# Another order of the first group's front in an attention and max-out kernel

## The chip, the cores and the metric

The kernel runs on one core of one Trainium2 chip. The metric is the device time of one execution in microseconds, from runs of the same compiled program; the median of the runs shown is compared. A profile of one execution lists each engine's instructions: TensorE (PE, with its weight loads as PEld), VectorE (DVE), ScalarE (ACT), GpSimd (POOL) and SyncE (SP), whose queue issues the transfers.

## The reference

q, k and v have the shape 8 x 8 x 576 x 64 (batch, heads, sequence, head size) in 32-bit floats. Attention is taken within chunks of 64 positions, and its output feeds a layer that takes the larger of three products:

```python
scores = scale * np.matmul(q_c, k_c.transpose(0, 1, 2, 4, 3))   # per chunk of 64
scores = scores - np.max(scores, axis=-1, keepdims=True)
attn = np.exp(scores)
attn = attn / (np.sum(attn, axis=-1, keepdims=True) + 1e-09)
out = np.matmul(attn, v_c)
x = out.transpose(0, 2, 1, 3).reshape(4608, 512)
h = np.maximum(np.maximum(x @ w1, x @ w2), x @ w3)              # w1..w3: 512 x 768
y = h @ w_out                                                   # w_out: 768 x 512
```

## The kernel before

The 4608 rows of x are cut into 36 tiles of 128 rows. Tiles 0 to 3 are the first group, 4 to 7 the second, and four units of 6, 8, 8 and 6 tiles follow. Matrix products are made from a high and a low part of each operand: three products (low x high, high x low, high x high, lines 187 to 189) add up in a bank of PSUM. The weights come in as 64-bit words and are converted on the chip into such a high and a low part.

The order of the first group's work, and of the second group's beginning, is written out by hand in the string `FIRST` (line 45). `first_group` walks through it and calls, for each name, the function that issues those instructions. An engine runs its own instructions in the order of the string; between engines the program puts waits where one reads or overwrites what another has written. What comes after the string is placed by a planner with due times, and by loops over the units.

The names, with t for a tile and jw for a piece of the weights (j is a block of 128 columns of the hidden layer, w one of the three matrices):

- `Wjw`, `qt`, `vt`: transfers on SP's queue. `Wjw` loads a piece of weights (512 KB), `qt` loads q and k of tile t (512 KB), `vt` its v (256 KB). A load waits until its buffer is free: q0, q3 and others share three buffers, `v0` and `v2` share one, as do `v1` and `v3`.
- `Ajw`, `Bjw`, `Cjw`, `Xjw`, `Hjw`, `Yjw`: the conversion of a piece. A (line 163) and B (line 168) run on ScalarE, C (line 172, a shift) on VectorE, X (line 176, an integer addition of what B and C left) on VectorE or, with a `p` behind the name, on GpSimd, H (line 179, the high part) on ScalarE, Y (line 182, the low part) on VectorE or, with `p`, on GpSimd.
- `St`: 32 products of 64 x 64 on TensorE, the scores of tile t (line 237). `mxt` (line 242) and `subt` (line 247) on VectorE take the maximum out of PSUM and subtract it; `expt` (line 251) runs on ScalarE; `sumt` (line 195), `epst` (line 198, adds 1e-9) and `rect` (line 201, the reciprocal) run on VectorE; `nrmt` (line 204) multiplies on VectorE or, with `p`, on GpSimd.
- `Tt`: four transposes on TensorE (line 260); `att` copies them on ScalarE (line 265); `Vt` multiplies with v on TensorE (line 296); `xht` (ScalarE, line 303) and `xlt` (VectorE, line 307) write the tile's high and low part of x.
- `hjwa`, `hjwb`, `hjwf`: twelve products of x with the converted piece, for the columns of tiles 0 and 1 (a), 2 and 3 (b) or all four (f). They need H and Y of the piece, and xh and xl of the tiles. `Fjwa` and so on (lines 349 and 351) take the larger of the results.
- `in`: n idle products on zeroed operands (line 795). They compute nothing that is used.

The scores of two tiles lie in one tile of PSUM, the outputs of V in another, with the tile's number inside and the half of the chunk outside:

```python
banks_of[name] = ps[name].tile([P, 2, 2, 4, 64], F32, name=name[-1])
st["s"] = s = bank_of("ps_s")[:, :, t % 2 if t < 4 or "pair" in st else 0]
```

so a tile's scores lie in both of its banks, in each beside those of the other tile. The pieces' words are placed by the order of the names in `FIRST`: `words_in` and `values_in` (lines 125 to 138) hand out rooms as W and A come, and take them back as X and Y come.

Of the kernel before, what the change touches and what calls it, by code (L numbers as in the profile page):

```python
# [42 lines left out]


FIRST = """
q0 i13 W01 A01 S0 i5 mx0 q1 sub0 W00 C01 exp0 sum0 S1 mx1 sub1 B01 q2 A00 exp1 W12 eps0 v0 q3 i8 rec0 B00 X01p S2 sum1
H01 mx2 eps1 nrm0p T0 at0 rec1 v1 sub2 nrm1p V0 T1 exp2 C00 S3 X00p xh0 q4 W02 at1 B12 sum2 H00 eps2 V1 rec2 mx3 xh1
nrm2p sub3 T2 S4 xl0 exp3 xl1 sum3 at2 Y00p v2 B02 W10 eps3 rec3 v3 nrm3 A02 W20 h00a V2 A12 C02 W31 T3 Y01p A10 xh2
X02 H02 at3 C10 W11 C12 X12p F00a h01a Y02 V3 xl2 B10 xh3 B31 q5 X10p xl3 A20 W21 A11 h02a F01a H12 F02a B11 C11 W61
W52 Z B20 B21 W40 H10 mx4 sub4 hh0a exp4 W22 C20 X20 W32 Y12 X11 Y10 A31 H11 W30 h01b hl0a h00b C31 h02b A21 H20 X31  # L50
S5 F00b C21 Y11 h12f F01b A40 q6 v4 H31 sum4 W41 B40 X21p h10f F02b H21 Y31 Y20 B30 hh0b eps4 hl0b Y21 C40 mx5 B61
X40p h11f h20f B32 F10f rec4 A22 sub5 W42 A32 C32 S6 A30 X32p h21f B22 W64 F11f F12f W51 C22 B52 H40 hh1f nrm4 hl1f
# [969 lines left out]
```

## Time and profile before

| | |
|---|---|
| median of 3 runs | 612.15 us (610.98 to 612.55) |
| profiled execution | 613.47 us |
| its span, first to last instruction | 611.7 us |
| TensorE busy | 600.5 us, 98% of the span |
| VectorE busy | 421.6 us, 69% |
| ScalarE busy | 290.4 us, 47% |
| GpSimd busy | 187.5 us, 31% |
| mean granted TensorE clock | 0.999 |
| transferred | 148.95 MB, mean 243 GB/s |

A row of a timeline gives the start in us from the span's start, the duration in us, the engine, the line of the kernel, the operation, what it writes and reads with the shapes, and how many instructions the row merges; in brackets stands the idle time of the engine ahead of it and what ended that. A row of the busy times by stretches gives the stretch, its length, then the busy time and the number of instructions of PE, PEld, DVE, ACT and POOL, the granted TensorE clock, the share of time in which the DMA engines were busy, and GB/s. A row of the transfers gives what is loaded, the queue, the count, the size, and the time from issue to landing in us.

### The profile page before, as it was taken

The numbers are of one execution on the slowest core, as the hardware profiler recorded it, in microseconds if no ns is written. First come the engines' busy times: TensorE is split into PE (matmuls) and PEld (weight loads), VectorE is DVE, ScalarE is ACT, GpSimd is POOL, SyncE is SP. The second block draws the span as 40 slices with busy tenths as digits, with TensorE's granted clock in tenths as the row PEclk, the third lists the DMA queues.
The fourth block names the chain that finished last, engine by engine and source line by source line (L and its number), as shares of the span: only waits on it lengthen the run. The fifth ranks groups of instructions, "written<-read, shape, count | busy, mean of one in ns | idle before, by whom it ended". The sixth has DMA issues, their size and how long they took to land.

```text
span 611.7 us, 12712 instructions
## 1 busy us (share of the span) xinstructions
PE 600.5 (98%) x5046; PEld 521.1 (85%) x5046; DVE 421.6 (69%) x700; ACT 290.4 (47%) x522; POOL 187.5 (31%) x168
## 2 busy tenths in 40 slices
PE   7899999999999999999999999999999999999997
PEld 3788878888799999997888878888888888999997
DVE  4898965768977986894674759936465598244373
ACT  4897734443454554555243344643333355333353
POOL 2522477777232424100250512002424000031300
PEclk9999999999999999999999999999999999999999
DMA  8987657755868998747796994468757543677532
GB/s 336 362 310 273 253 190 274 271 204 234 313 227 287 348 333 312 275 134 266 248 313 239 328 289 163 148 235 280 253 193 259 179 155 114 225 253 261 197 129 79
DMA packets 59483, 148.95 MB, mean 243 GB/s; under 512 B 5664, under 2 KB 24608, under 8 KB 59424
## 3 DMA queue, kind: packets, MB, share of 16 engines
q1 hardware_dynamic: 59424, 148.13, 69.0%
q8 instruction: 40, 0.66, 0.4%
q14 instruction: 19, 0.16, 0.1%
HBM read 116.92 MB, written 31.20 MB: 242 GB/s over the span
## 4 chain that ended last, share of the span: by engine, by line
PE 84%; DVE 7%; DMA 3%; ACT 2%; POOL 2%; issue 1%; SPq 0%; DVEq 0%; ACTq 0%; POOLq 0%
PE pm L187 26%; PE pm L189 26%; PE pm L188 26%; PE s L237 2%; PE pm L296 2%; POOL c L420 2%; DMA buf<-in_vb 2%; DMA e<-b 1%; PE tp L260 1%; PE pm L795 1%; DVE e L247 1%; DVE sm L195 1%; DVE s L428 1%; DVE h L361 1%; DVE mx L242 1%
## 5 line engine op out<-in xcount | busy, mean ns | idle before, releaser
L187 PE MATMUL pm<-X,ring 128*128 128x512 f32 (+1 forms) x504 | 184.3, 366 | 0.3 <-ACT kept L626 0.3
L189 PE MATMUL pm<-X,ring 128*128 128x512 f32 (+1 forms) x504 | 182.5, 362 | 0.5 <-issue 0.5
L188 PE MATMUL pm<-X,ring 128*128 128x512 f32 (+1 forms) x504 | 182.4, 362 | 0.0
L626 ACT COPY kept<-pm 128x384 f32<-128x384 f32 (+1 forms) x144 | 76.9, 534 | 156.6 <-PE pm L189 154.9
L187 PEld LDWEIGHTS pm<-X,ring 128*128 128x128 f32 x504 | 94.6, 188 | 11.2 <-ACT kept L626 0.7
L189 PEld LDWEIGHTS pm<-X,ring 128*128 128x128 f32 x504 | 94.6, 188 | 10.7 <-issue 0.8
L188 PEld LDWEIGHTS pm<-X,ring 128*128 128x128 f32 x504 | 94.7, 188 | 9.7
L632 POOL TENSOR_TENSOR kept<-kept 128x384 f32<-128x384 f32 (+1 forms) x24 | 29.0, 1208 | 129.2 <-ACT kept L626 129.2
L629 DVE TENSOR_TENSOR pm<-pm,kept 128x384 f32<-128x384 f32 (+1 forms) x48 | 30.0, 626 | 51.4 <-PE pm L189 51.4
L187 PE MATMUL pm<-xh,wl 128*128 128x512 f32 (+1 forms) x156 | 60.0, 385 | 0.0
L188 PE MATMUL pm<-xl,wh 128*128 128x512 f32 (+1 forms) x156 | 58.4, 374 | 0.3 <-DVE xl L307 0.3
L189 PE MATMUL pm<-xh,wh 128*128 128x512 f32 (+1 forms) x156 | 58.3, 374 | 0.0
L594 DVE TENSOR_TENSOR H<-most,H 128x384 fp32r<-128x384 f32 (+1 forms) x72 | 48.5, 687 | 11.1 <-ACT H L591 11.0
L635 DVE TENSOR_TENSOR most<-pm,most 128x384 f32<-128x384 f32 (+1 forms) x72 | 44.6, 619 | 10.8 <-PE pm L189 9.4
L204 POOL TENSOR_TENSOR e<-e,sm 128x512 f32<-128x512 f32 x27 | 31.3, 1161 | 63.6 <-ACT kept L626 18.9
L242 DVE TENSOR_REDUCE mx<-s 128x8 f32<-128x512 f32 x36 | 24.6, 683 | 36.9 <-PE s L237 36.9
L632 POOL TENSOR_TENSOR most<-kept 128x384 f32<-128x384 f32 (+1 forms) x12 | 13.8, 1150 | 115.8 <-ACT kept L626 115.8
L591 ACT CAST H<-most 128x384 fp32r<-128x384 f32 (+1 forms) x72 | 40.6, 569 | 10.5 <-PE pm L189 9.0
L528 DVE TENSOR_TENSOR X<-stage,X 128x768 fp32r<-128x768 f32 (+1 forms) x28 | 34.0, 1222 | 13.1 <-ACT X L524 13.0
L524 ACT CAST X<-stage 128x768 fp32r<-128x768 f32 (+1 forms) x28 | 26.3, 945 | 28.1 <-DVE stage L519 22.0
L251 ACT ACTIVATE e<-e 128x512 f32<-128x512 f32 x36 | 22.8, 633 | 27.9 <-DVE e L247 27.9
L189 PE MATMUL pm<-H,woh 128*128 128x384 f32 (+1 forms) x96 | 34.7, 362 | 0.0
(119 smaller groups left out, 1062.8 us busy)
## 6 DMA issues: line engine op xcount, KB each, us to landing
ring<-w SPq DMA_DIRECT2D x72, 768.0 KB, 6.0
buf<-in_qk SPq DMA_DIRECT2D x36, 512.0 KB, 6.2
buf<-in_vb SPq DMA_DIRECT2D x36, 256.0 KB, 6.8
ring<-w SPq DMA_DIRECT2D x36, 256.0 KB, 4.1
w<-s SPq DMA_DIRECT2D x9, 768.0 KB, 3.8
out_x<-ao SPq DMA_DIRECT2D x24, 256.0 KB, 3.0
ring<-wo SPq DMA_DIRECT2D x8, 768.0 KB, 5.0
stage<-in_w SPq DMA_DIRECT2D x7, 512.0 KB, 6.4
```

The lines of the kernel that those rows point to most:

```text
L187: nc.tensor.matmul(out=o, lhsT=al, rhs=bh, start=first, stop=False, skip_group_check=shared)
L188: nc.tensor.matmul(out=o, lhsT=ah, rhs=bl, start=False, stop=False, skip_group_check=shared)
L189: nc.tensor.matmul(out=o, lhsT=ah, rhs=bh, start=False, stop=last, skip_group_check=shared)
L204: eng.tensor_tensor(out=e, in0=e, in1=sm.unsqueeze(2).broadcast_to([P, 8, 64]), op=ALU.mult)
L242: nc.vector.tensor_reduce(out=st["mx"].rearrange("p (g c) -> p c g", c=2), in_=st["s"], axis=AX.X, op=ALU.max)
L528: return lambda: eng.tensor_tensor(out=X[i][:, 1], in0=source[i](), in1=X[i][:, 0].bitcast(F32), op=minus)
L591: nc.scalar.copy(out=H[i, jp][:, 0, :half], in_=hidden_block(i, jp))
L594: nc.vector.tensor_tensor(out=H[i, jp][:, 1, :half], in0=hidden_block(i, jp), in1=H[i, jp][:, 0, :half].bitcast(F32), op=minus)
L626: return lambda: nc.scalar.copy(out=to, in_=o)
L629: return lambda: nc.vector.tensor_tensor(out=o if w else M(jp, q), in0=o, in1=kept(k), op=plus)
L632: nc.gpsimd.tensor_tensor(out=kept(3) if w else M(jp, A22), in0=kept(3), in1=kept(p7), op=plus)
L635: return lambda: nc.vector.tensor_tensor(out=M(jp, q), in0=of, in1=M(jp, q), op=most)
```

## The change

The four lines at the head of `FIRST` are written anew; the rest of the string and all functions stay as they are.

```diff
 FIRST = """
-q0 i13 W01 A01 S0 i5 mx0 q1 sub0 W00 C01 exp0 sum0 S1 mx1 sub1 B01 q2 A00 exp1 W12 eps0 v0 q3 i8 rec0 B00 X01p S2 sum1
-H01 mx2 eps1 nrm0p T0 at0 rec1 v1 sub2 nrm1p V0 T1 exp2 C00 S3 X00p xh0 q4 W02 at1 B12 sum2 H00 eps2 V1 rec2 mx3 xh1
-nrm2p sub3 T2 S4 xl0 exp3 xl1 sum3 at2 Y00p v2 B02 W10 eps3 rec3 v3 nrm3 A02 W20 h00a V2 A12 C02 W31 T3 Y01p A10 xh2
-X02 H02 at3 C10 W11 C12 X12p F00a h01a Y02 V3 xl2 B10 xh3 B31 q5 X10p xl3 A20 W21 A11 h02a F01a H12 F02a B11 C11 W61
+W01 q0 i13 A01 B01 q1 C01 X01 W00 H01 Y01 S0 i2 S1 i3 mx0 sub0 q2 A00 exp0 mx1 v0 sum0 eps0 rec0 S2 nrm0p sub1 q3 B00
+exp1 i4 C00 X00p W12 T0 sum1 at0 eps1 rec1 v1 nrm1p S3 H00 mx2 V0 W02 xh0 sub2 T1 exp2 Y00p q4 at1 xl0 mx3 V1 B12 sum2
+xh1 eps2 rec2 nrm2p sub3 xl1 T2 A02 S4 exp3 at2 h00a B02 sum3 v2 C02 W10 eps3 rec3 v3 nrm3 V2 X02 W20 F00a h01a xh2 H02
+T3 A12 W31 xl2 Y02 at3 A10 C10 W11 C12 X12p V3 xh3 B10 B31 q5 X10p xl3 A20 W21 A11 h02a F01a H12 F02a B11 C11 W61
 W52 Z B20 B21 W40 H10 mx4 sub4 hh0a exp4 W22 C20 X20 W32 Y12 X11 Y10 A31 H11 W30 h01b hl0a h00b C31 h02b A21 H20 X31
 S5 F00b C21 Y11 h12f F01b A40 q6 v4 H31 sum4 W41 B40 X21p h10f F02b H21 Y31 Y20 B30 hh0b eps4 hl0b Y21 C40 mx5 B61
 X40p h11f h20f B32 F10f rec4 A22 sub5 W42 A32 C32 S6 A30 X32p h21f B22 W64 F11f F12f W51 C22 B52 H40 hh1f nrm4 hl1f
```

From `B31` on both orders agree. By engine, the orders up to there are these (before, then after):

```
SP    q0 W01 q1 W00 q2 W12 v0 q3 v1 q4 W02 v2 W10 v3 W20 W31 W11
      W01 q0 q1 W00 q2 v0 q3 W12 v1 W02 q4 v2 W10 v3 W20 W31 W11
ACT   A01 exp0 B01 A00 exp1 B00 H01 at0 exp2 xh0 at1 B12 H00 xh1 exp3 at2 B02 A02 A12 A10 xh2 H02 at3 F00a B10 xh3
      A01 B01 H01 A00 exp0 B00 exp1 at0 H00 xh0 exp2 at1 B12 xh1 A02 exp3 at2 B02 F00a xh2 H02 A12 at3 A10 xh3 B10
DVE   mx0 sub0 C01 sum0 mx1 sub1 eps0 rec0 sum1 mx2 eps1 rec1 sub2 C00 sum2 eps2 rec2 mx3 sub3 xl0 xl1 sum3 eps3 rec3 nrm3 C02 X02 C10 C12 Y02 xl2
      C01 X01 Y01 mx0 sub0 mx1 sum0 eps0 rec0 sub1 C00 sum1 eps1 rec1 mx2 sub2 xl0 mx3 sum2 eps2 rec2 sub3 xl1 sum3 C02 eps3 rec3 nrm3 X02 xl2 Y02 C10 C12
POOL  X01 nrm0 nrm1 X00 nrm2 Y00 Y01 X12
      nrm0 X00 nrm1 Y00 nrm2 X12
PE    i13 S0 i5 S1 i8 S2 T0 V0 T1 S3 V1 T2 S4 h00a V2 T3 h01a V3
      i13 S0 i2 S1 i3 S2 i4 T0 S3 V0 T1 V1 T2 S4 h00a V2 h01a T3 V3
```

The first piece of weights, W01, is loaded ahead of q0 and converted ahead of tile 0's maximum, its X and Y on VectorE in place of GpSimd. The scores of tiles 0 and 1 stand together ahead of that maximum. Each eps and rec stands directly behind its sum. 22 idle products stand in place of 26.

## The prediction

> **What bounds the kernel now.** I read the page's busy shares first, then busy time by stretches, then the timeline of the front engine by engine, then the issue and landing of the first transfers.
>
> ```profile
> PE 600.5 (98%) x5046; PEld 521.1 (85%) x5046; DVE 421.6 (69%) x700; ACT 290.4 (47%) x522; POOL 187.5 (31%) x168
> ```
>
> ```profile
> 6.90:27.32 20.42, 16.71 (x355) 12.47 (x354) 16.95 (x33) 14.64 (x27) 11.25 (x9) 1.00 0.96 370
> 27.32:611.70 584.38, 578.05 (x4679) 506.81 (x4679) 404.40 (x667) 273.78 (x494) 175.32 (x152) 1.00 0.69 239
> ```
>
> TensorE bounds the whole: from 27.32 us on it is busy 578.05 of 584.38. Only before that does anything else rule, so the change is worth the moment at which TensorE runs without gaps, counted against the work left. That moment is the second product of step h01b:
>
> ```profile
> 25.12 0.39 PE L187 MATMUL pm<-xh,wl 128*128 128x256 f32 x1
> ...
> 26.66 0.33 PE L187 MATMUL pm<-xh,wl 128*128 128x256 f32 x1
> 27.32 0.38 PE L188 MATMUL pm<-xl,wh 128*128 128x256 f32 x1 [0.34 <-DVE xl L307]
> ```
>
> The twelve products of h02a take 1.54 us (25.12 to 26.66), 0.13 each. The second product of h01b waits until 27.32; without that wait h01b would have begun at 27.32 - 0.13 = 27.2. I carry the changed front to the same place and compare.
>
> Up to there VectorE leads. Its first instructions follow one another almost without idle time (mx0, sub0, C01, sum0, then eps1, rec1, sub2, C00, sum2, eps2, rec2):
>
> ```profile
> 7.61 0.69 DVE L242 TENSOR_REDUCE mx<-s 128x8 f32<-128x512 f32 x1 [6.47 <-PE s L237]
> 8.33 0.69 DVE L247 TENSOR_TENSOR e<-s,mx 128x512 f32<-128x512 f32 x1
> 8.94 0.42 DVE L172 TENSOR_SCALAR ao<-ao 128x512 uint32<-128x512 uint32 x1
> 9.72 0.69 DVE L195 TENSOR_REDUCE sm<-e 128x8 f32<-128x512 f32 x1 [0.36 <-ACT e L251]
> ...
> 13.63 0.16 DVE L198 TENSOR_SCALAR sm<-sm 128x8 f32<-128x8 f32 x1
> 13.82 0.20 DVE L201 RECIPROCAL sm<-sm 128x8 f32<-128x8 f32 x1
> 13.99 0.69 DVE L247 TENSOR_TENSOR e<-s,mx 128x512 f32<-128x512 f32 x1
> 14.60 0.89 DVE L172 TENSOR_SCALAR ao<-ao 128x512 uint32<-128x512 uint32 x1
> 15.44 0.69 DVE L195 TENSOR_REDUCE sm<-e 128x8 f32<-128x512 f32 x1
> 16.16 0.78 DVE L198 TENSOR_SCALAR sm<-sm 128x8 f32<-128x8 f32 x1
> 16.98 0.20 DVE L201 RECIPROCAL sm<-sm 128x8 f32<-128x8 f32 x1
> ```
>
> From these starts come my steps: 0.72 to a VectorE instruction that needs the one before (7.61 to 8.33), 0.61 to one that doesn't (8.33 to 8.94), 0.19 from eps to rec, 0.17 from rec to the next. Two shapes stand twice with different times: the shift C takes 0.42 and then 0.89, the guard eps 0.16 and then 0.78. The long ones end as a GpSimd instruction ends:
>
> ```profile
> 14.17 1.04 POOL L204 TENSOR_TENSOR e<-e,sm 128x512 f32<-128x512 f32 x1 [1.00 <-DVE sm L201]
> 15.63 1.29 POOL L176 TENSOR_TENSOR ao<-ao,xh 128x512 int32<-128x512 int32 x1 [0.42 <-ACT e L251]
> ```
>
> C00 ends at 15.49, 0.28 after nrm1 (15.21); eps2 ends at 16.94, X00p at 16.92. So C and eps on VectorE stand still while GpSimd works; sum2 (0.69 beside X00p) does not.
>
> TensorE in the same stretch (thirteen idle products, S0, idle, S1, idle, S2, T0, V0):
>
> ```profile
> 1.19 5.72 PE L795 MATMUL pm<-h 128*128 128x512 bf16 x13 [1.19 <-DVE h L797]
> 6.84 0.69 PE L237 MATMUL s<-buf 64*64 64x64 f32 x32
> 7.47 1.25 PE L795 MATMUL pm<-h 128*128 128x512 bf16 x5
> 9.08 0.69 PE L237 MATMUL s<-buf 64*64 64x64 f32 x32 [0.35 <-DVE e L247]
> 9.70 1.90 PE L795 MATMUL pm<-h 128*128 128x512 bf16 x8
> 11.78 0.69 PE L237 MATMUL s<-buf 64*64 64x64 f32 x32 [0.18 <-DVE e L247]
> 13.22 0.66 PE L260 MATMUL tp<-ident,e 128*128 128x128 f32 x4 [0.74 <-POOL e L204]
> 14.55 0.69 PE L296 MATMUL x<-xs,buf 64*64 64x64 f32 x32 [0.68 <-ACT xs L265]
> ```
>
> S1 starts as sub0 ends (9.02), though S1 writes tile 1's half of s and sub0 reads tile 0's; S2 waits for sub1 likewise. Both halves of s share banks (c is the outer index), and the program keeps readers and writers of a bank in the order in which they are written. That is the row on which the forecast hangs. [...] By that rule the new order, S1 ahead of mx0, makes mx0 wait for S1; by addresses alone it would not, which is rival A.
>
> **The change part by part.** No instruction goes but four idle products (26 to 22). X01 and Y01 move from GpSimd to VectorE; the rest is order.
>
> Transfers: W01 is issued first, then q0; W00, q2 keep their places; v0 and q3 go ahead of W12, v1 and W02 ahead of q4.
>
> ```profile
> 0.74 0.38 SPq L225 DMA_DIRECT2D buf<-in_qk  x1
> ...
> 1.65 0.42 SPq L225 DMA_DIRECT2D buf<-in_qk  x1
> 2.11 0.43 SPq L154 DMA_DIRECT2D xh<-in_w  x1
> 2.59 0.71 SPq L225 DMA_DIRECT2D buf<-in_qk  x1
> ```
>
> Time from issue to landing of the first, third, fourth and fifth of these transfers:
>
> ```profile
> buf<-in_qk SPq DMA_DIRECT2D x1, 512.0 KB, 3.7
> buf<-in_qk SPq DMA_DIRECT2D x1, 512.0 KB, 6.2
> xh<-in_w SPq DMA_DIRECT2D x1, 512.0 KB, 7.1
> buf<-in_qk SPq DMA_DIRECT2D x1, 512.0 KB, 7.8
> ```
>
> q1 lands at 1.65 + 6.2 = 7.85, W00 at 9.2, q2 at 10.4, and all three are unmoved. W01 and q0 have equal bytes and swap: W01 lands at 0.74 + 3.7 = 4.45, and q0 when W01 did, just ahead of ScalarE's A01:
>
> ```profile
> 5.67 0.66 ACT L163 ACTIVATE ao<-xh 128x512 f32<-128x512 f32 x1 [3.65 <-DMA xh<-in_w]
> 9.06 0.63 ACT L251 ACTIVATE e<-e 128x512 f32<-128x512 f32 x1 [2.73 <-DVE e L247]
> ```
>
> So q0 is there by 5.7, and S0 is held by the thirteen idle products till 1.19 + 5.72 = 6.9 as before: no cost. A01, B01, X01, H01, Y01 in turn, at A01's 0.66 each, end at 4.45 + 5 x 0.66 = 7.75. VectorE idles there anyway, so this conversion is free, unless it passes mx0's start.
>
> Taken off the VectorE chain: C01 from between sub0 and sum0. Worth 0.1 only: sum0 waits for exp0 at 9.72 whether C01 stands there or not, and mx1 now fills the hole.
>
> Added: mx0 behind S1. S1 starts after S0 (7.53) and two idle products: 7.53 + 2 x 0.25 = 8.03, with q1 there at 7.85. S0's first row starts 0.77 before mx0, so mx0 comes at 8.75 to 8.8, not 7.61: **+1.15 us**.
>
> From there (starts; GpSimd in brackets): mx0 8.75, sub0 9.47, mx1 10.08, exp0 10.20, sum0 10.86, eps0 11.58, rec0 11.77, [nrm0 12.05 to 13.09], sub1 11.94. S2 now stands ahead of sub1 and behind mx1 in the banks: 10.8, q2 just landed, done 11.5, no wait. exp1 12.67. C00 at 12.55 meets nrm0 and ends 0.28 behind it, 13.37. sum1 13.33. [X00p 13.5 to 14.8.] eps1, now directly behind sum1, at 14.05, meets X00p and ends with it: 14.83 instead of 14.21, **0.6 us** that eps1 did not pay before (eps2 did). rec1 14.85, [nrm1 15.1 to 16.15], mx2 15.02, sub2 15.74, xl0 16.35, exp2 16.47, mx3 16.96, sum2 17.57, eps2 18.29 ([Y00p] over by 17.5, so 0.16), rec2 18.48 (before: 16.98). So the chain stays late by its first 1.15; C01 gone and eps1's stall even out against eps2's stall gone; xl0 and mx3, which stood behind rec2, now stand ahead of it.
>
> TensorE follows rec2: nrm2 18.76 to 19.80, T2 19.86, S4 20.5, h00a 21.15 (xl0, xl1 and Y00 done by 20.0), V2 22.7, h01a 23.4, T3 24.9. T to V is 1.33 (13.22 to 14.55), with the copy between, and nothing now lies under it: V3 26.2, h02a 26.9, h01b 26.9 + 1.54 = 28.4. xl3 is done by 28.3, so the wait of 27.32 is gone. **28.4 - 27.2 = +1.2 us.**
>
> Behind that, queues: v3 waits for V1 and W20, W31, W11 stand behind it on SP, about 1 us later; their readers on ScalarE are later too, so nothing. C11 may now meet X10p on GpSimd, and would stand still for at most X00p's 1.29; the products of h02a and h01b (2 x 1.54) lie over it, so I take 0 of 0 to 1.29. The fewer idle products: 0, bounded below.
>
> Ends: without the hold and eps1's stall +0.15 (rival A); with a W01 that lands as late as before (5.67), Y01 ends at 9.0, +0.25, and with C11's 1.29 on the path the sum is +2.75. It runs from +0.15 to +2.75; I take +1.2, by the S1 row. Against the profiled execution: span 611.7 + 1.2 = 612.9. That execution's 613.47 stands 0.2% above the median of the runs shown, 612.15, so the median becomes 613.35, forecast 613.3.
>
> **The rivals.** A, no hold: mx0 at Y01's 7.75. Then exp0 stands behind A00, which needs W00 at 9.2: exp0 9.75, not 10.20. Gain 0.45, so +0.75: 612.9; with eps1's stall gone too, +0.15: 612.3, no change. Against it: the S1 and S2 rows.
>
> B, faster: A, and also V3's gap filled (T3 to V3 1.33, with 0.66 of it the transpose): another 0.7 off, h01b at 26.6, -0.6: 611.55. For a gain of 1.84 (0.3%) the front would have to end by 25.4, and no row gives that.
>
> C, slower: TensorE drops to its slow rate. The first idle products took 0.44 each (6.91 - 1.19 over 13), the five at 7.47 0.25. Between V0's end near 15.2 and T2 at 19.9 only T1 and V1 run, 1.35 of 4.7 us, sparser than any such stretch before. If it slowed there, T2, S4, h00a and V2, 3.6 us, would take up to 0.76 of it more (0.44 to 0.25): +2.7 at most, half of it likely: 614.65; it decides once more than 0.65 is lost. Against: the longest gap is about 1.5 us, and the stretch before at 12.5 to 14.5 was sparse without harm. [...]
>
> **How the numbers follow.** 0.3% (1.84 us) is about what a measurement of this kernel can tell from no change. Forecast 0.6 (own range 612.3 to 614.9; same 0.52, slower 0.08); A 0.18 (same); B 0.1 (same 0.04, faster 0.06, for what my walk overlooks); C or a late conversion 0.12 (slower 0.11, same 0.01). Sums: faster 0.06, same 0.75, slower 0.19. The range takes in A and B's near end below and half of C above: 611.2 to 615.2.
>
> **What would show it.** In the profile after: mx0 starting behind S1 near 8.75; eps1 long and ending with X00p, eps2 short; T2 near 19.9; V3 waiting for at3; h01b running without a wait near 28.4, and equal waits after it. mx0 at 7.8 shows A; products of h00a over 0.2 us apart show C; h01b under 27 proves the walk wrong.

## The result and the profile after

The changed kernel takes 614.39 us (median of five runs, 614.25 to 614.71) against 612.15 of the kernel before (five runs, 610.98 to 612.55): a ratio of 1.0053, 95% interval 1.0040 to 1.0066. It is 2.2 us slower, where 613.3 and no measurable change were forecast. The profiled execution is the one of 614.25; its span is 612.5. Two executions among the experiments below took 996 and 1211 us (last section) and are left out of the medians.

The page of the changed kernel, first the busy shares and then the granted clock in 40 slices:

```profile
PE 600.0 (98%) x5041; PEld 522.3 (85%) x5042; DVE 423.0 (69%) x702; ACT 290.4 (47%) x522; POOL 184.1 (30%) x166
PEclk9799999999999999999999999999999999999999
```

TensorE bounds the whole as before, but the second slice (15.3 to 30.6 us) has a 7 in the clock. Busy time by stretches of 1 us, TensorE alone (stretch, length, busy time and count, granted clock, DMA share, GB/s), shows when:

```profile
17.00:18.00 1.00, 0.69 (x32) 1.00 0.90 358
18.00:19.00 1.00, 0.00 (x0) 0.78 0.25 90
19.00:20.00 1.00, 0.55 (x3) 0.50 0.88 246
...
24.00:25.00 1.00, 1.00 (x23) 0.50 1.02 401
25.00:26.00 1.00, 1.00 (x28) 0.81 1.00 410
26.00:27.00 1.00, 1.00 (x11) 1.00 1.03 418
```

By the shares in these rows the clock was halved (0.50) from 18.56 to 25.38, for 6.8 us. TensorE's timeline in that place, after and then in a second trace of the kernel before (before_again, below):

```profile
15.85 0.66 PE L260 MATMUL tp<-ident,e 128*128 128x128 f32 x4 [1.14 <-POOL e L204]
17.21 0.69 PE L296 MATMUL x<-xs,buf 64*64 64x64 f32 x32 [0.71 <-ACT xs L265]
19.45 1.12 PE L260 MATMUL tp<-ident,e 128*128 128x128 f32 x4 [1.55 <-POOL e L204]
20.50 1.13 PE L237 MATMUL s<-buf 64*64 64x64 f32 x32
21.56 0.58 PE L187 MATMUL pm<-xh,wl 128*128 128x256 f32 x1
21.94 0.41 PE L188 MATMUL pm<-xl,wh 128*128 128x256 f32 x1
...
24.42 1.11 PE L296 MATMUL x<-xs,buf 64*64 64x64 f32 x32
25.46 0.39 PE L187 MATMUL pm<-xh,wl 128*128 128x256 f32 x1
...
28.33 0.69 PE L296 MATMUL x<-xs,buf 64*64 64x64 f32 x32 [0.73 <-ACT xs L265]
...
35.95 0.47 PE L187 MATMUL pm<-xh,wl 128*128 128x512 f32 x1 [0.36 <-DVE wl L182]
```

```profile
6.09 0.69 PE L237 MATMUL s<-buf 64*64 64x64 f32 x32
...
17.69 0.66 PE L260 MATMUL tp<-ident,e 128*128 128x128 f32 x4 [1.16 <-POOL e L204]
18.28 0.69 PE L237 MATMUL s<-buf 64*64 64x64 f32 x32
18.93 0.39 PE L187 MATMUL pm<-xh,wl 128*128 128x256 f32 x1
...
20.56 0.69 PE L296 MATMUL x<-xs,buf 64*64 64x64 f32 x32
...
31.55 0.50 PE L187 MATMUL pm<-xh,wl 128*128 128x512 f32 x1
```

From T2 to V2's end the same work takes 6.01 us after (19.45 to 25.46, where h01a follows) and 3.58 before (17.69 to 21.27, the end of V2 there): T2 and S4 1.05 and 1.06 instead of 0.59 and 0.65, products of h00a 0.21 apart instead of 0.12. That is 2.4 us. After it the clock is full and both run alike, up to the first product over four tiles (step h12f, the last row of each), which I take as the front's end from here on: 35.95 after, 31.55 in before_again.

VectorE's timeline after (Y01, mx0, eps1, eps2, rec2):

```profile
6.94 0.69 DVE L182 TENSOR_TENSOR wl<-ao,wh 128x512 fp32r<-128x512 f32 x1 [0.68 <-ACT wh L179]
8.19 0.69 DVE L242 TENSOR_REDUCE mx<-s 128x8 f32<-128x512 f32 x1 [0.56 <-PE s L237]
...
13.54 0.82 DVE L198 TENSOR_SCALAR sm<-sm 128x8 f32<-128x8 f32 x1
...
17.78 0.17 DVE L198 TENSOR_SCALAR sm<-sm 128x8 f32<-128x8 f32 x1
17.98 0.20 DVE L201 RECIPROCAL sm<-sm 128x8 f32<-128x8 f32 x1
```

Tile 0's scores are there at 6.6, but mx0 stands behind Y01, which ends at 7.63, and then waits 0.56 for TensorE's S1. eps1 is the long one and ends with X00p (13.05 to 14.34 on GpSimd), eps2 is short.

**The front in numbers.** Starts read off the same rows of each trace (mx0 L242, rec2 the third L201, T2 the third L260, h12f the first 512-column L187):

| kernel | mx0 | mx0 to rec2 | T2 | T2 to h12f | h12f |
|---|---|---|---|---|---|
| before, the profile of the prediction | 7.61 | 9.37 | 18.45 | 13.88 | 32.33 |
| before_again | 6.85 | 9.37 | 17.69 | 13.86 | 31.55 |
| after | 8.19 | 9.79 | 19.45 | 16.50 | 35.95 |
| after_again | 8.18 | 9.79 | 19.44 | 16.16 | 35.60 |
| e1b_warm | 8.84 | 9.78 | 20.09 | 13.98 | 34.07 |
| e5_warm_t3 | 8.52 | 9.79 | 19.78 | 13.44 | 33.22 |
| e6_warm_apart | 8.07 | 9.43 | 19.21 | 13.91 | 33.12 |
| e13_pair_warm | 7.80 | 9.38 | 18.65 | 13.91 | 32.56 |
| e14_warm_same_length | 8.38 | 10.33 | 20.18 | 13.97 | 34.15 |
| e15_undone_same_length | 8.44 | 9.43 | 19.34 | 13.46 | 32.80 |

Against before_again the changed front is 4.40 us late: 1.34 by a later mx0, 0.42 between mx0 and rec2, 2.64 from T2 on. (From rec2 to T2 both take 1.47.)

**Part of that comes back.** TensorE's busy time behind the front (stretch, length, busy time), before_again and then after:

```profile
186.00:230.00 44.00, 43.59 (x596) 1.00 0.95 339
230.00:372.00 142.00, 141.06 (x1269) 1.00 0.78 264
```

```profile
186.00:230.00 44.00, 44.00 (x606) 1.00 0.92 326
230.00:372.00 142.00, 141.67 (x1279) 1.00 0.78 268
```

The kernel before, which comes there sooner, loses 0.41 and 0.94 us, the changed one 0 and 0.33. The rows of before_again at the idle places say why:

```profile
189.71 0.44 PE L189 MATMUL pm<-X,ring 128*128 128x384 f32 x1 [0.41 <-issue]
...
357.23 1.10 PE L296 MATMUL pm<-e,buf 64*64 64x64 f32 x29 [0.47 <-DMA e<-b]
```

The TensorE that arrives sooner waits once with "issue", that is, for nothing that the profile shows (the experiments come back to it), and once for a transfer; the one that comes 4 us later waits for neither. The lag of the same VectorE instructions is 4.8 us at 34, 4.1 at 200, 3.5 at 300 and 2.6 from 367 to the end, and 2.7 us is what the spans differ by (612.5 and 609.8).

### The profile page after: what moved, and what is told of

It is laid out like the page before. It is cut to its first block, busy times and chain, and to the rows that moved or that the text cites. A ratio compares the mean times of both kernels' runs of the same rounds, so it can differ in the third digit from the quotient of the medians.

```text
span 612.5 us, 12705 instructions
## 1 busy us (share of the span) xinstructions
PE 600.0 (98%) x5041; PEld 522.3 (85%) x5042; DVE 423.0 (69%) x702; ACT 290.4 (47%) x522; POOL 184.1 (30%) x166
## 4 chain that ended last, share of the span: by engine, by line
PE 85%; DVE 5%; DMA 2%; POOL 2%; ACT 1%; issue 1%; SPq 0%; POOLq 0%; ACTq 0%; DVEq 0%
PE pm L187 27%; PE pm L188 26%; PE pm L189 26%; PE pm L296 2%; PE s L237 2%; POOL c L420 2%; PE tp L260 1%; DMA xh<-in_w 1%; DVE s L428 1%; DVE h L361 1%; DMA w<-s 1%; DMA xl<-in_w 1%; ACT s L425 1%; DVE X L528 0%; PE s L296 0%
## 5 line engine op out<-in xcount | busy, mean ns | idle before, releaser
L187 PE MATMUL pm<-X,ring 128*128 128x512 f32 (+1 forms) x504 | 184.5, 366 | 0.3 <-ACT kept L626 0.3
L187 PEld LDWEIGHTS pm<-X,ring 128*128 128x128 f32 x504 | 94.6, 188 | 11.3 <-ACT kept L626 0.9
L187 PE MATMUL pm<-xh,wl 128*128 128x512 f32 (+1 forms) x156 | 60.6, 388 | 0.4 <-DVE wl L182 0.4
L242 DVE TENSOR_REDUCE mx<-s 128x8 f32<-128x512 f32 x36 | 24.6, 684 | 28.2 <-PE s L237 28.2
L187 PEld LDWEIGHTS pm<-xh,wl 128*128 128x128 f32 x156 | 29.9, 192 | 5.9 <-PE s L237 0.5
```

The costliest lines, as they stand in the source:

```text
L187: nc.tensor.matmul(out=o, lhsT=al, rhs=bh, start=first, stop=False, skip_group_check=shared)
```

## The experiments

In the strings, `lN` stands for N idle products on 32-bit operands with 256 columns. "Clock full" means a mean granted clock of 0.999 or 1.000 in that execution, "fallen" one of 0.991 to 0.997. Each comparison is with the kernel before on the same chip.

**Fewer idle products in the old order** (18 instead of 26).

```diff
-A01 S0 i5 mx0 ... v0 q3 i8 rec0
+A01 S0 i2 mx0 ... v0 q3 i3 rec0
```

> The kernel before, with two and three idle products where it had five and eight, its order untouched. Theory 'clock': the idle products keep TensorE at its full clock; with fewer of them a stretch at half clock appears in the front and the time rises by 1 to 2.5 us, to 613.2 to 614.7. Rival 'order': idle products change nothing as long as nothing waits for them: 612.15, within 0.4.

611.46 (11 runs) against 610.62, ratio 1.0010 (0.9994 to 1.0027). But the runs fall apart by the clock: seven at full clock have a median of 609.94, four with a fallen clock 612.55. In the trace the clock was halved from 13.3 to 20.1. So with fewer idle products the clock falls in some executions, and those are 2.6 us longer here. The kernel before, with all 26, keeps the full clock in each of the 111 executions that were timed beside the experiments, on five chips.

**The pair alone** in the old order: S0 and S1 together ahead of mx0, nothing else.

```diff
-A01 S0 i5 mx0 q1 sub0 ... sum0 S1 mx1
+A01 S0 q1 i2 S1 i3 mx0 sub0 ... sum0 mx1
```

> The kernel before with one part of the change alone: S1 right behind S0 (two idle products between), both ahead of mx0. Theory 'hold': mx0 waits for S1 and comes 0.6 to 1.1 us later, the VectorE chain with it, and the time rises by as much, to 612.7 to 613.3. Rival 'absorbed': mx1 in the hole behind sub0 gives it back: 612.15, within 0.4.

612.97 (12 runs) against 610.62, 1.0030 (1.0017 to 1.0044). mx0 came at 7.80, 0.95 later than in before_again, with the hold behind S1; the clock fell in nine of twelve executions (median 613.31; the three full ones 612.25). All 26 idle products are there: the order alone can bring the fall.

**The conversion alone** in the old order.

```diff
-q0 i13 W01 A01 S0
+W01 q0 i13 A01 B01 C01 X01 H01 Y01 S0
```

> The kernel before with one part of the change alone: W01 loaded ahead of q0 and converted ahead of mx0, its X and Y on VectorE. Theory 'start': mx0 now stands behind Y01, which ends at 7.6 whatever the idle products do, and S0 behind a q0 that lands later: mx0 at 7.65, 0.3 to 1.3 us later than in a typical execution of the kernel before; C01 gone gives 0.1 back: the time rises by 0.3 to 1.0. Rival 'cover': VectorE idles there, so the conversion is free and one piece less to convert later makes the front 0.3 to 0.8 us shorter.

610.92 (11 runs) against 610.87, 1.0003 (0.9994 to 1.0012): no change in time, as the prediction's step had it. It is not free in the front, though: in the trace mx0 starts at 7.49, behind Y01, 0.64 later than in before_again, and the clock fell in five of the eleven executions (median 611.60; the full ones 610.68).

**More idle products in the new order** (33): the clock kept up.

```diff
-xh0 sub2 T1 ... xl0 mx3 V1 ... sub3 xl1 T2
+xh0 sub2 i4 T1 ... xl0 mx3 i2 V1 ... sub3 xl1 i5 T2
```

> The changed kernel with eleven more idle products in the three gaps of TensorE behind V0: four ahead of T1, two ahead of V1, five ahead of T2. Theory 'clock': most of the loss is TensorE at half its clock from 18.6 to 25.4 us, because it had too little to do from 15.1 to 18.6; then no stretch at half clock is left, the products of h00a stand 0.12 us apart instead of 0.21, V2 follows T2 about 2.4 us sooner, and the time falls from 614.4 to 612.0 (611.5 to 612.5). Rival 'order': the slow products have another cause, or are covered, and the waits of the new order make up the loss; then the time stays at 614.4.

> The changed kernel with eleven more idle products behind V0 once more, for a profile at full clock. Theory 'clock': granted clock 0.999 or above, products of h00a 0.12 us apart, the wait-free run of TensorE from h02a on begins some 2.3 us sooner than in the changed kernel's profile (28.95 to about 26.6), and the time is 2 us or more below the changed kernel's on this chip. Rival 'order': the sooner start is given back before 60 us, in waits for converted weights, and the time is level.

Both are the same kernel, on two chips. The clock stayed full in nine of the ten executions counted, and the time did not follow: 613.93 against 610.62, 1.0050 (1.0036 to 1.0064); and 613.60 against 610.96, 1.0048 (1.0031 to 1.0064). Two rows of the second one's timeline of TensorE:

```profile
20.09 0.66 PE L260 MATMUL tp<-ident,e 128*128 128x128 f32 x4 [0.36 <-POOL e L204]
...
191.82 0.34 PE L189 MATMUL pm<-X,ring 128*128 128x384 f32 x1 [1.20 <-issue]
```

From T2 to h12f it needs 13.98 instead of 16.16, as much as the kernel before, so the fall had cost 2.2 there; the front as a whole ends 1.5 sooner than in after_again (34.07 and 35.60). But at 190 us TensorE now stands still for 1.20 with "issue", where the changed kernel has no stop. In this trace most of what had been won was lost in that place (spans 612.3 and 612.4).

**Whether more idle products alone bring that stop**: the old order with 7 more (33).

```diff
-eps1 nrm0p T0 ... sub2 nrm1p V0 ... nrm2p sub3 T2
+eps1 nrm0p i3 T0 ... sub2 nrm1p i2 V0 ... nrm2p sub3 i2 T2
```

> The kernel before with seven more idle products, placed into waits of TensorE ahead of T0, V0 and T2, so that nothing in the front moves by more than 0.1 us and TensorE's program is as long as in the two warm kernels that stood still near 190 us. Theory 'fetch': the stop near 190 us (1.2 and 1.3 us in them, no engine to wait for) is TensorE running out of fetched instructions, and the fourteen added instructions put it into this kernel too: 0.8 to 1.4 us near 190, the time up by as much. Rival: no stop, or the 0.5 of the kernel before, and the time within 0.3.

> The kernel before, unchanged, for a second profile of it. Theory 'start': the thirteen idle products ended at 5.5 to 6.6 us in the four profiles of the second call, as the clock rose at another moment in each; in the profile at hand of the kernel before they ended at 6.9, the latest. The old order starts mx0 right behind S0, so a typical execution has mx0 at 6.3 to 7.3 instead of 7.61, its chain on VectorE as much sooner, and no waits of TensorE on transfers after 200 us: span 608 to 610. Rival 'as seen': mx0 at 7.6 again.

611.96 against 610.87, 1.0019 (1.0011 to 1.0028), for e7; 611.02, 1.0006 (0.9995 to 1.0018), for the kernel before run once more with a trace. The fronts are equal (h12f at 31.50 and 31.55); e7's stop at 190 us is the longest of the traces:

```profile
189.40 0.45 PE L188 MATMUL pm<-X,ring 128*128 128x384 f32 x1 [1.53 <-issue]
```

In the prediction's profile of the kernel before a transfer on the queue of instructions begins at 187.94, 2.4 before the end of its stop of 0.51, at 190.38. From 186 to 192 before_again (stop 0.41) and e1b_warm (1.20) have one such transfer, e7 (1.53) two. The page of the changed kernel counts these transfers, 40 of them with 0.66 MB, so 16.5 KB each:

```profile
q8 instruction: 40, 0.66, 0.4%
```

In the changed kernel's trace the transfer begins at 191.69, and TensorE does not stop at all. A TensorE that had run out of instructions would fit all this; the traces do not name who reads that queue, so it is the author's guess and not shown. The stop goes with the number of products in TensorE's program (5046 on the page of the kernel before, and from there by the idle products of each edit): the traces with 5038 to 5043 show none there, those with 5046 0.41 to 0.51 or none, those with 5051 to 5053 0.47 to 1.53.

**The changed kernel once more**, beside e1b_warm.

> The changed kernel itself, beside the next three on one chip, so that the price of the slow stretch is measured on equal terms. Theory 'clock': 2 us or more above the next run, with a granted clock of 0.994 to 0.997 in most executions. Rival 'order': level with the next run, within 0.5.

613.78 (five runs) against 610.96, 1.0050 (1.0038 to 1.0063); clock halved from 17.7 to 24.6 in the trace and below full in all five executions, no stop at 190.

**Single holds undone, on top of e1_warm.** First mx0 ahead of S1:

```diff
-S0 i2 S1 i3 mx0 sub0 q2
+S0 i5 mx0 sub0 S1 q2
```

> The kernel of the first run of this call (changed order, eleven more idle products) with mx0 and sub0 ahead of S1, so that mx0 need not wait for S1. Theory 'hold': mx0 starts behind Y01, about 0.5 us sooner, and the time is 0.5 us below that of the first run. Rival 'absorbed': exp0 waits for A00 and S2 for q2 as before, and the time is the first run's, within 0.2.

613.73 against 610.62, 1.0051 (1.0038 to 1.0063): nothing gained. Its timeline, TensorE's S1 and VectorE's first instructions:

```profile
7.61 0.69 DVE L242 TENSOR_REDUCE mx<-s 128x8 f32<-128x512 f32 x1
...
9.08 0.69 PE L237 MATMUL s<-buf 64*64 64x64 f32 x32 [0.35 <-DVE e L247]
9.84 0.69 DVE L242 TENSOR_REDUCE mx<-s 128x8 f32<-128x512 f32 x1 [0.82 <-PE s L237]
```

mx0 no longer waits, S1 then waits for sub0, and mx1 for S1 (0.82): the wait has moved by one tile, and sub1 comes at 11.49 instead of 11.35. Then T3 and its copy ahead of h01a:

```diff
-F00a h01a xh2 H02 T3 A12 W31 xl2 Y02 at3 A10
+F00a T3 h01a xh2 H02 at3 A12 W31 xl2 Y02 A10
```

> The kernel of the run before this one with T3 ahead of h01a again and the copy of T3 (at3) ahead of A12, as the kernel before had it. Theory 'gap': the 0.7 us that TensorE waits for that copy between T3 and V3 lie under h01a; V3 follows h01a without idle time and the time falls by 0.7 (0.5 to 0.9). Rival 'conversion': TensorE then waits as much longer for Y12 ahead of h12f (0.4 in the changed kernel), and the time falls by 0.3 at most.

613.66 against 610.96, 1.0050 (1.0036 to 1.0064). V3 has lost its wait and T2 to h12f is 0.54 shorter than in e1b_warm, but not the time; h12f's wait for Y12 is up from 0.38 to 0.59. The stop at 190 is only 0.47 and the traced execution, 612.34, is the fastest of the five: what made the others longer is not in the trace. Then eps1 kept apart from X00p:

```diff
-C00 X00p W12 T0 sum1 at0 eps1 rec1 v1 nrm1p S3 H00 mx2 V0 ... exp2 Y00p q4 at1 xl0
+C00 W12 T0 sum1 at0 S3 mx2 eps1 rec1 v1 nrm1p X00p V0 ... exp2 q4 at1 H00 xl0 ... nrm2p Y00p
```

> The kernel of the second run with one part of the change undone: mx2 stands between sum1 and eps1, and X00 behind nrm1 on GpSimd (H00 behind at1, Y00 behind nrm2, as they have to), so that eps1 meets no work on GpSimd. Theory 'port': eps1 takes 0.17 instead of 0.82, mx2 comes a microsecond sooner, T2 0.7 to 1.0 sooner, and the time falls by as much. Rival: Y00, now behind nrm2, or the conversion of W12 holds TensorE instead, and the time is level, within 0.3.

613.59 against 610.96, 1.0045 (1.0032 to 1.0058). VectorE, mx2 and eps1:

```profile
13.91 0.69 DVE L242 TENSOR_REDUCE mx<-s 128x8 f32<-128x512 f32 x1 [0.53 <-PE s L237]
14.52 0.16 DVE L198 TENSOR_SCALAR sm<-sm 128x8 f32<-128x8 f32 x1
```

eps1 takes 0.16 instead of 0.82, but mx2 in front of it waits 0.53 for S2 and S3: from mx0 to rec2 it is 9.43 instead of 9.78, 0.35 won. The stop at 190 was 1.30.

**Warm with fewer, longer products.** The new order with `l1`, `l1`, `l2` in place of i2, i3, i4, and `l2`, `l1`, `l2` where e1_warm has its own; then the same with the edits of e5 and e6.

> The changed kernel kept warm without a longer program: nine idle products on 32-bit zeros of 256 columns (each about 0.43 us, as long as two of the others) in the gaps behind S0, S1, S2, V0, T1 and V1, in place of the nine short ones, so that TensorE's program has the changed kernel's length. Theory 'clock and fetch': full clock, no stop near 190 us, and the time 1.0 to 1.8 us below the changed kernel's 2.8 above before, so 1.0 to 1.8 above before. Rival 'order': level with the changed kernel, 2.6 to 2.8 above before.

> The kernel of the run before this one with two parts of the order undone as well: mx2 between sum1 and eps1 with X00 behind nrm1, and T3 ahead of h01a. What is left of the change is the early load and conversion of W01 and the pair of scores. Theory: each gave its 0.7 to 0.8 us in the front, so the front is 1.0 to 1.5 us shorter than in the run before and the time 0.2 to 0.8 above before. Rival 'given back': TensorE, sooner, meets the waits on transfers after 200 us that the kernel before meets, and gains 0.5 at most over the run before.

613.50 against 610.93, 1.0046 (1.0030 to 1.0063), and 613.33, 1.0038 (1.0025 to 1.0051). They miss their purpose: the trace counts each 32-bit idle product as two, so both have 5051 products and stops of 1.48 and 1.30 at 191. In e11 the front is only 1.0 behind before_again (h12f at 32.58), and the kernel is 2.4 us slower all the same.

**The pair alone, kept warm**, in the old order:

```diff
-S0 i5 mx0 q1 sub0 ... sum0 S1 mx1 ... q3 i8 rec0 ... nrm0p T0 ... nrm1p V0 ... nrm2p sub3 T2
+S0 q1 l1 S1 l5 mx0 sub0 ... sum0 mx1 ... q3 rec0 ... nrm0p l1 T0 ... nrm1p l1 V0 ... nrm2p sub3 l1 T2
```

> The kernel before with S1 behind S0 and ahead of mx0, as in the third run of the first call, but kept warm by nine long idle products in TensorE's gaps (none added in number). Theory 'hold': full clock, mx0 behind S1 at 7.8 to 8.8 instead of 6.9 to 7.6, the front 0.6 to 1.2 us longer, the time 0.3 to 1.0 above before. Rival 'absorbed': the hole behind sub0, now filled with mx1, gives it back: within 0.3.

612.96 against 610.93, 1.0040 (1.0027 to 1.0053); at full clock 612.6 (the median of eight). The front is 1.0 late, all of it mx0's 0.95, and the stop 1.08. So the hold costs the front 1 us. The stop could be the rest of the 1.7, but e3, the same order without a stop at 190 in its trace, is 1.6 above before at full clock (three executions).

**The same number of products as in the changed kernel, spread** (22):

```diff
-q0 i13 ... S0 i2 S1 i3 mx0 ... exp1 i4 C00 ... sub2 T1 ... mx3 V1 ... xl1 T2
+q0 i10 ... S0 i2 S1 i2 mx0 ... exp1 i1 C00 ... sub2 i3 T1 ... mx3 i1 V1 ... xl1 i3 T2
```

> The changed kernel with its 22 idle products spread otherwise: ten ahead of S0, two and two behind S0 and S1, one ahead of T0, three ahead of T1, one ahead of V1, three ahead of T2. TensorE's program has the changed kernel's 5041 products. Theory 'clock and fetch': full clock in most executions, no stop near 190 us, and 0.9 to 1.6 us above before where the changed kernel stood 2.2 to 2.8 above. Rival 'order': 2.4 to 2.8 above before all the same.

The second kernel has, besides, the edits of e5 and e6:

> The kernel of the run before this one with mx2 between sum1 and eps1, X00 behind nrm1, and T3 ahead of h01a. Theory: 0.5 to 1.0 us below the run before, so 0 to 0.8 above before, without a stop near 190 us. Rival 'pair': the early scores and the early conversion, the parts still there, hold 2 us or more above before by themselves.

e14: 613.81 (seven runs) against 610.95, 1.0049 (1.0029 to 1.0070). e15: 612.41 (twelve), 1.0019 (1.0007 to 1.0032), which is 1.5 above before where 0 to 0.8 was expected. Neither has a stop at 190. But spreading did not hold the clock: it fell in six of e14's seven executions, in its trace earlier:

```profile
10.00:11.00 1.00, 0.55 (x20) 0.66 0.96 371
...
17.00:18.00 1.00, 0.94 (x6) 0.92 0.90 291
```

There, ahead of T2, it lengthens mx0 to rec2 by 0.54 and little else. h12f is 1.45 sooner than in after_again, the span 0.7 shorter (611.7 and 612.4), and the median not at all. e15 stayed at full clock in four of twelve executions: 611.53 with it, 612.68 without, 1.15 apart.

**The old order with a shorter start**: e9 has i10 for i13; e12 has that and `l2`, `l4` for i5, i8.

> The kernel before with ten idle products ahead of S0 instead of thirteen. Theory 'start': the old order's chain begins with S0, which the idle products hold; S0 and mx0 come 0.6 to 1.3 us sooner (q0 lands at 4.5) and the time falls by 0.3 to 1.0, unless the clock rises later. Rival: A00 and S2 stand behind W00 (9.2) and q2 (10.4) and take the gain back: within 0.2.

> The kernel before with ten idle products ahead of S0 and, in place of the five and the eight behind S0 and S1, two and four of the long ones: a program of TensorE twenty instructions shorter. Theory 'start and fetch': the start as in the run with ten (0.5 to 1.1 us sooner), the stop near 190 us (0.4) gone, full clock: 1.0 to 1.6 us below before. Rival: fewer products let the clock fall, as with two and three: 0.5 to 2.5 above.

e9: 609.78 (11 runs) against 610.87, 0.9988 (0.9975 to 1.0001), the best of all, though its interval touches no change; no stop at 190 (5043 products), clock full in ten of eleven. Its mx0 at 6.75 is hardly sooner than before_again's 6.85, so the gain, if it is one, is not shown to come from the start. e12: 611.32, 1.0006 (0.9991 to 1.0021); its clock fell in eight of twelve.

## Why the prediction was wrong

**What held.** mx0 waits for S1 (0.56), so the order by banks holds, on which the forecast hung, and rival A is out. eps1 is long and ends with X00p, eps2 short: mx0 to rec2 is 9.79, predicted 9.73. T2 at 19.45 (predicted 19.86), V3 waiting for at3 (0.73), h01b without a wait. The conversion costs no time (e8).

**The step that failed** is the walk of TensorE from T2 to h01b, taken at full speed: "The fewer idle products: 0, bounded below", and with it rival C's 0.12. No run shows that 0; the trace of the changed kernel shows 2.4 us in its place. The forecast put T2 to h01b at 8.5 us (19.86 to 28.4). It took 11.0 (h01b's first product is at 30.49), because TensorE ran at half clock, as rival C described: h00a's products 0.21 apart. C put the most that it could cost at 2.7 us of the front; the trace has 2.4, and 2.2 by e1b_warm. I argued against it from the longest gap of about 1.5 us, and the gaps were as long as I said (1.14, 0.71, 1.55); no run shows how long a gap has to be for the clock to fall. But their sum is what the trace shows around the fall: from V0's end to T2 (14.71 to 19.45) TensorE is busy 1.35 of 4.74 us (T1 and V1). In the profile of the kernel before it is busy 1.98 of 3.21 us between the same two (15.24 to 18.45), as S3 still stands between T1 and V1 there; the changed order has it ahead of V0. So it is the rearranged work, and not only the four products fewer, that left the stretch empty; e3 and e8 fall with all 26. No gap was longer than 1.55 us, and the clock fell all the same, in all five timed runs.

**A term mis-sized by its base.** mx0's delay was put at 1.15, taken from a profile of before whose mx0 at 7.61 was itself late: in before_again it is 6.85, and e9 has 6.75. The thirteen idle products end at a different moment in each trace (S0 at 5.51 in after_again, 6.85 in e1b_warm), the old order's mx0 follows S0 at once, and the new order's cannot: it stands behind Y01, which ends at 7.63, and behind S1, which needs q1. The delay is 0.6 against the one trace and 1.3 against the other. Of the 1.3, up to 0.78 is Y01 (6.85 to 7.63), which the prediction called free unless it passes mx0's start: in an execution with an early S0 it does.

**What was left out.** That a later TensorE meets fewer waits behind the front: 1.0 of the 4.4 us come back by the idle time in the two stretches shown, 1.7 by the spans. And that idle products lengthen the program: this doesn't touch the changed kernel, which has four products fewer, but with seven more in the old order the time rose by 1.1 us (e7), and that is part of why warming gave no time.

**What a fall costs at the end.** Six kernels have several executions at full clock and several with a fallen one, and in each the median with the fall is longer: by 0.9 us in e8, 1.1 in e3, 1.15 in e15, 1.8 in e13, 2.1 in e12 and 2.6 in e2. The changed kernel's clock fell in all ten of its executions, the kernel before's in none of 111. So the fall costs time, and the forecast had it at nothing.

**How the loss is made up.** By e14 and e15, kernels of one length: 0.6 us stay with e15 at full clock (611.53 against 610.95), where mx0 is still late; 1.2 lie between the two at fallen clock (613.86 and 612.68), which is eps1 with X00p and T3 behind h01a; and 1.15 is the fall itself in e15. Together they are e14's 2.9, where after_again lost 2.8. This is a split of e14, whose clock falls earlier than the changed kernel's, and other runs give other shares: the pair alone at full clock is 1.6 above before (e3), and e5 and e6 gained nothing by undoing T3 or eps1 alone. Executions of the kernel before alone reach from 609.1 to 613.5. So the shares stay rough.

**Open.** What the clock's fall in the place of the changed kernel costs at the end, at equal program length and with nothing else altered: no run with 22 products held the clock reliably. The fall's length does not settle it either. A mean clock of 0.997 means half as long at half clock as 0.994 (an estimate: 0.003 and 0.006 of 612 us, doubled, are 3.7 and 7.3). The changed kernel's two executions at 0.997 took 614.30 and 614.39, the three at 0.994 614.25 to 614.71; in after_again three at 0.996 and 0.997 took 613.30 to 613.78, two at 0.994 614.17 and 614.69. Nor is it settled what keeps the clock up. e3's clock fell behind gaps of TensorE of 1.77, 0.74 and 0.67 us (ahead of S2, T0 and V0), e2's behind 1.26 and 0.74 (ahead of S2 and T0); before_again, with gaps of up to 1.16 (ahead of T2) behind its first S0, keeps it. But e15's trace has gaps of 1.60, 1.40 and 0.81 (ahead of S2, T0 and T1), and its clock stayed full.

## What to carry to other kernels

Idle products are part of the timing: before taking any away, or moving work out from between them, count what TensorE is still busy with in a sparse stretch (here 1.35 of 4.74 us between V0's end and T2 where the clock fell, 1.98 of 3.21 where it did not), and ask what would then run at half speed. Adding them can have a price far off: seven to eleven more went with a stop of 0.47 to 1.53 us at 190 us. And take the base of a sum from several executions: a start that varies by 0.8 us decides whether a hold costs 0.6 or 1.3.

## What was not expected of the hardware

- In the changed kernel the clock fell with no gap over 1.55 us, and stayed down for 6.8 us though TensorE was busy throughout from 19.45 on, 0.89 behind the fall. In e3 and e8, where it was busy from the fall on, the clock was back after 3.4 us (15.02 to 18.44 and 14.50 to 17.92).
- One execution of e1_warm took 1211 us, its products of 128x256 on lines 188 and 189 at 0.45 us in the mean, where the changed kernel's took 0.41 at half clock and 0.28 at full, though its granted clock reads 1.00; one of e2_fewer_idle, with a mean clock of 0.557, took 996 us.
- TensorE stopped for up to 1.53 us at 190 us, in the prediction's profile of the kernel before until 2.4 us after a transfer of 16.5 KB on the queue of instructions began; with five to seven products more than the kernel before in the first 20 us the stop was 0.47 to 1.53, with as many as before 0 to 0.51.
- A 32-bit idle product counts as two in the trace: e10, with 13 short ones and nine of these, has 5051 products, the kernel before with 26 short ones 5046.
